# Linear attention and a mixture of experts on one core: attention in plain fp32 on halves of the tensor engine, and experts whose second layer runs five chunks behind the first

## The chip, the core and the metric

The kernel runs on one core of a Trainium2 chip. The metric is device microseconds from start to end of the program, smaller is better. A core has a tensor engine (PE) whose loads of the stationary operand stand as a row of their own (PEld), a vector engine (DVE), a scalar engine (ACT), GpSimd (POOL), and a sync engine (SP) that here issues most DMAs. Each engine works through its own instructions in order; semaphores hold them together.

## The reference

Two stages. Attention with a feature map: for 8 batches and 8 heads of 576 tokens by 64, both q and k become 256 features, exp(p) and exp(-p) of a projection p less its largest magnitude; no softmax over tokens.

```python
def phi(x):
    proj = np.einsum('bhsd,df->bhsf', x, w_phi)                 # 64 -> 128
    proj = proj - np.max(np.abs(proj), axis=-1, keepdims=True)
    return np.concatenate([np.exp(proj), np.exp(-proj)], axis=-1)
q_p, k_p = (phi(q), phi(k))
kv = np.einsum('bhsf,bhsd->bhfd', k_p, v)
z = np.sum(k_p, axis=2)
num = np.einsum('bhsf,bhfd->bhsd', q_p, kv)
den = np.einsum('bhsf,bhf->bhs', q_p, z)[..., None] + 1e-06
out = num / den
```

The result, as 4608 tokens of 512, goes through 8 experts, each token through one: the expert whose normalised embedding has the largest dot with the normalised token. The output is `gate * (relu(x @ w1[e]) @ w2[e])` with w1 512 x 1024, w2 1024 x 512, and gate the softmax weight of that expert. All in fp32.

## The kernel before

**Attention** runs in 16 quads: a quad is four heads of one batch, as two pairs (`X`) of two heads (`e`). The two heads of a pair lie on the two halves of the partitions, and the tokens of both pairs beside each other, 1152 columns or 9 blocks of 128. Matmuls with large outputs use fp32r operands, a rounded format that the tensor engine takes in one pass; to keep fp32's accuracy each operand is split into a rounded part (`h`) and what that leaves (`l`), and three products h·h, h·l, l·h are summed. So raw q, k, v and the key features kp are split: the rounding by ACT (L203) or DVE (L206), the rest by POOL or DVE (L197). In quad j:

- `proj` (L229): a block's projections for both heads of a pair at once, three fp32r products of 256 columns. DVE takes the largest magnitude (L233) and subtracts it (L235).
- For k, ACT makes the two exponentials (L242), then `split_k` splits them. For q, `qtr` turns the shifted projections on the tensor engine (L257), ACT makes the exponentials (L260).
- `kv` (L282): [v 1]ᵀ·kp, three fp32r products for each of five blocks; ACT copies it to SBUF (L285); `kve` (L296) turns it back with the identity and multiplies it with the embeddings in the same matmul, in fp32; DVE copies (L298).
- `num` (L310, L313): the numerators, the denominators and the dots with the embeddings of each block of tokens, plain fp32: 128 query features as the stationary operand, 73 columns. `norm` divides (L338 to L344), and writes x to DRAM.

Queue order is written out by hand for PE (`frame`); a scheduler orders the other engines. Numerators run a quad behind.

**Routing** (`route`, L405 to L443) counts the tokens of each expert and scatters them into a table, for groups of two batches beside the attention; the last group's runs after it, beside the first expert unit.

**Experts** run in 17 units, each of 2 slots of 128 tokens of one expert (3 in the first and in an expert's first unit where the number of slots is odd; 1 where the expert has one slot). Which code a unit runs is read from a table on the chip: `units` makes for every unit a Switch of 12 arms, each arm unrolled for one number of tokens, with or without the loads of the next expert. At a unit's end every engine loads the next arm's number (L132 on PE) and branches. In a unit `layers` goes through 8 chunks of 128 hidden features: `layer1` (L688, 12 fp32r matmuls of the unit's tokens), ACT's relu (L690) and DVE's rest (L693) into `hh`, `hl`, and one chunk later `layer2` (L711, three matmuls of 512 columns for each slot). A unit's tokens come by indirect DMA (`gather_parts`, L604), are turned by DVE (L617) and split (`xsplit`, L203, L648). The next expert's weights are split in the last unit of an expert (`next_w1`, `next_w2`, L584). A unit of one slot has its own code, `layers_of_slot` (L765, L774).

## Time and profile before

| | us |
|---|---|
| median of 3 runs (lowest, highest) | 1102.26 (1091.81, 1107.28) |
| the profiled execution, first to last instruction | 1133.1 |
| busy in it: PE, PEld | 965.3, 860.1 |
| busy in it: DVE, POOL, ACT | 651.2, 538.0, 433.5 |
| from its start to the first expert matmul | 516.1 |
| from there to the last expert matmul's end | 602 |

The profiled execution is a single one and is 2.8% longer than the median of the runs. Busy times of PE are modelled, since matmuls are pipelined: a matmul's row lasts from its start to the end of its result, so that neighbours overlap, and the distance of two starts is what one costs in a run of them. A plain fp32 matmul leaves two rows of LDWEIGHTS and MATMUL, an fp32r one a single row: `num`'s L310 stands in the program 512 times and has 992 rows with the tile np and 32 with bk. In brackets stands the idle time ahead of a row and what ended it; "issue" is a wait for nothing that the profile shows.

### The profile page before, as it was taken

What the parts mean: (1) busy time and instruction counts of PE and PEld (TensorE: products, weight loads), DVE (VectorE), ACT (ScalarE), POOL (GpSimd) and SP (SyncE); (2) the same over time, 40 slices, a digit from 0 to 9 for tenths busy, and PEclk for the clock granted to TensorE, in tenths of its full rate; (3) what the DMA queues carried; (4) which work ended last, traced back from release to release, by engine and by line L of the source; (5) the groups of instructions that cost most, each with busy time, mean ns of one, the idle gap of its engine ahead of it and who ended that gap; (6) DMA issues with size and microseconds to landing.
All of it is one profiled execution on the core that took longest, in us unless ns stands there. A gap on an engine that the chain in (4) does not pass through costs nothing. (4 is left out here: it accounts for less than half of the span.)

```text
span 1133.1 us, 17328 instructions
## 1 busy us (share of the span) xinstructions
PE 965.3 (85%) x6188; PEld 860.1 (76%) x6188; DVE 651.2 (57%) x1289; ACT 433.5 (38%) x841; POOL 538.0 (47%) x396
## 2 busy tenths in 40 slices
PE   6999999999899989988898788698687588798874
PEld 4899888888788878877787677587576477687763
DVE  8888898989899898969221223324225623422221
ACT  5556554645354554543221223314225413312221
POOL 5555564776477664655433224325144454422322
PEclk7999998999899999989899888799788778899887
DMA  5223221313132224111611111514313531511111
GB/s 166 83 66 106 61 88 46 105 51 106 63 105 66 79 90 180 45 29 43 215 37 49 38 40 49 191 23 126 106 45 116 159 123 46 188 28 45 47 35 43
DMA packets 55822, 94.22 MB, mean 83 GB/s; under 512 B 22471, under 2 KB 22855, under 8 KB 55440
## 3 DMA queue, kind: packets, MB, share of 16 engines
q1 hardware_dynamic: 45808, 68.97, 19.2%
q0 software_dynamic: 9632, 21.32, 6.3%
q14 instruction: 285, 2.33, 0.7%
q8 instruction: 97, 1.59, 0.7%
HBM read 70.64 MB, written 19.96 MB: 80 GB/s over the span
## 5 line engine op out<-in xcount | busy, mean ns | idle before, releaser
L604 POOL DMA_INDIRECT xg<-xd,ix x156 | 152.6, 978 | 260.2 <-DVE xt L617 168.5
L693 DVE SCALAR_TENSOR_TENSOR hl<-bk,hh 128x256 fp32r<-128x256 f32 (+2 forms) x128 | 57.6, 452 | 340.9 <-ACT hh L690 275.9
L197 POOL TENSOR_TENSOR kpl<-kp,kph 128x1024 fp32r<-128x1024 f32 (+1 forms) x79 | 170.1, 2153 | 121.3 <-DVE kph L206 111.7
L688 PE MATMUL bk<-xh,w1h 128*128 128x256 f32 (+4 forms) x512 | 169.5, 331 | 61.6 <-issue 54.2
L690 ACT ACTIVATE hh<-bk 128x256 fp32r<-128x256 f32 (+4 forms) x128 | 52.6, 415 | 346.4 <-PE bk L688 248.7
L688 PEld LDWEIGHTS bk<-xh,w1h 128*128 128x128 f32 x512 | 111.2, 217 | 73.4 <-issue 60.7
L688 PE MATMUL bk<-xl,w1h 128*128 128x256 f32 (+4 forms) x512 | 166.6, 325 | 0.0
L688 PE MATMUL bk<-xh,w1l 128*128 128x256 f32 (+4 forms) x512 | 165.9, 324 | 0.0
L260 ACT ACTIVATE qp<-bk 128x512 f32<-128x512 f32 (+1 forms) x160 | 79.9, 552 | 148.0 <-PE bk L257 134.5
L310 PE MATMUL np<-kvs,qp 128*128 128x73 f32 x992 | 126.1, 283 | 0.0
L310 PEld LDWEIGHTS np<-kvs,qp 128*128 128x128 f32 x992 | 124.2, 203 | 0.1
L688 PEld LDWEIGHTS bk<-xl,w1h 128*128 128x128 f32 x512 | 111.7, 218 | 4.9
L233 DVE TENSOR_REDUCE m<-bk 128x4 f32<-128x512 f32 (+1 forms) x157 | 98.9, 632 | 28.4 <-PE bk L229 22.6
L206 DVE CAST kph<-kp 128x1024 fp32r<-128x1024 f32 (+1 forms) x77 | 109.7, 1424 | 6.6 <-ACT kp L242 6.1
L688 PEld LDWEIGHTS bk<-xh,w1l 128*128 128x128 f32 x512 | 110.9, 217 | 0.0
L242 ACT ACTIVATE kp<-kd 128x512 f32<-128x512 f32 (+1 forms) x160 | 83.6, 580 | 50.2 <-DVE kd L235 49.5
L823 POOL DMA_INDIRECT out<-o,ent x39 | 41.0, 1052 | 95.5 <-ACT o L817 88.6
L711 PE MATMUL bk<-w2h,hh 128*128 128x512 f32 x136 | 59.7, 439 | 31.2 <-ACT hh L690 23.2
L711 PE MATMUL np<-w2h,hl 128*128 128x512 f32 (+1 forms) x160 | 65.7, 411 | 0.0
L711 PE MATMUL np<-w2h,hh 128*128 128x512 f32 (+1 forms) x160 | 65.4, 409 | 0.0
L711 PE MATMUL np<-w2l,hh 128*128 128x512 f32 (+1 forms) x160 | 65.2, 408 | 0.0
L257 PE MATMUL bk<-cst,qd 128*128 128x128 f32 x288 | 50.3, 296 | 8.9 <-DVE qd L235 8.9
(248 smaller groups left out, 2210.6 us busy)
## 6 DMA issues: line engine op xcount, KB each, us to landing
w1r<-w SPq DMA_DIRECT2D x14, 1024.0 KB
w2r<-w SPq DMA_DIRECT2D x14, 1024.0 KB
q<-qT SPq DMA_DIRECT2D x16, 576.0 KB
k<-kT SPq DMA_DIRECT2D x15, 576.0 KB
xd<-x SPq DMA_DIRECT2D x8, 1024.0 KB
va<-va SPq DMA_DIRECT2D x16, 325.0 KB
va<-va SPq DMA_DIRECT2D x16, 260.0 KB
xg<-xd,ix POOLq DMA_INDIRECT x156
```

The costliest lines, as they stand in the source:

```text
L197: ins = eng.tensor_tensor(out=hl[1], in0=raw, in1=hl[0].bitcast(F32), op=ALU.subtract)
L206: self.v.tensor_copy(out=out, in_=in_)
L233: v.tensor_reduce(out=m, in_=pv, axis=AX.X, op=ALU.max, apply_absolute_value=True)
L242: nc.scalar.activation(out=k[:, :nu, s], in_=d[:, :nu], func=AF.Exp, scale=sc)
L257: nc.tensor.transpose(out=ps[:, e, c, :], in_=self.dq[g][:, c, e, :], identity=self.ident)
L260: nc.scalar.activation(out=q[:, s, :, :nu], in_=ps[:, :, :nu], func=AF.Exp, scale=sc)
L310: nc.tensor.matmul(out=n[:, i * W:(i + 1) * W], lhsT=self.qp[g][:, s, e, c], rhs=self.kvs[j][:, X, e, s], start=(s == 0), stop=(s == 1))
L604: ins = nc.gpsimd.indirect_dma_start(out=self.xg[i][:, q * P:(q + 1) * P], out_offset=None, in_=self.xd.rearrange("n (g d) -> (n g) d", g= ...
L688: nc.tensor.matmul(out=ps, lhsT=w[:, d, fs], rhs=x[:, d, :n], start=(d == 0 and i == 0), stop=(d == 3 and i == 2))
L690: high = nc.scalar.activation(out=hh[:, :n], in_=ps, func=AF.Relu)
L693: low = self.v.scalar_tensor_tensor(out=out, in0=ps[:, cs], scalar=0.0, in1=hh[:, cs].bitcast(F32), op0=ALU.max, op1=ALU.subtract)
L711: self.nc.tensor.matmul(out=self.acc[a // P][:b - a], lhsT=h[:, a:b], rhs=w[:, c], start=(c == 0 and i == 0), stop=(c == 7 and i == 2))
```

## The change

Attention no longer splits anything. Every matmul of it takes plain fp32 operands and uses half of the array:

- `proj` works a head at a time: 64 rows of the array (partitions 0 to 63 for one head, 64 to 127 for the other), the two heads in turn, each into a PSUM bank of its own, 128 columns. A quad's 18 blocks go in five steps (`step`), over two pairs of banks.
- `kv` has the key features as the stationary operand, 64 of their 128 columns at a time, so that the outputs fall to partitions 0 to 63 and 64 to 127 in turn; moving are v, the ones, and v's products with the embeddings. These come from `vemb`, a new step (20 small matmuls a quad over a new input vT), copied by ACT into the tile `va`. `kve` and the copy `kt` go.
- `num` takes 64 tokens at a time in the same way. `norm` has one operation where it had two for the full and the half block.
- `split`, `split_v`, `split_k` and their work on ACT, DVE and POOL go. The loads of a quad are q, k, vT and va (zero padded to ten blocks of 73 columns). Of a batch pair's squares one more is taken; emb and tau are loaded by ACT's queue; table scatters and splits of the early expert's weights wait for DVE's latest subtraction.

In the experts every chunk has its own `hs` pair (three tiles and five that attention leaves), x has two sets, layer 1 goes round five PSUM banks, and `layer2` runs five chunks behind (`LAG`). An arm ends after chunk 4 of layer 2 (and, for a third slot, all chunks); chunks 5 to 7 of the first two slots and their outputs are in `unit_end`, code that is the same after every arm. It begins with the load of the next arm's number and a hint (`switch_hint`) that names the coming branch. A one-slot unit has no code of its own: it takes 256 columns in layer 1. The second half of w2 is split in an expert's first unit. There are 14 arms. Small `idle` instructions make the arms' counts equal. ACT, DVE, POOL and SP of the later units now stand in the written order too.

```diff
-    def split_k(self, g, copy=None, eng=None):
-        nu = GR[g][1]
-        k = self.kf[g][:, :nu]
-        hl = self.kp[g] = [t[:, :nu] for t in (self.pa.tile([P, 2, 2, 2, P], F32R, name="kp" + i, bufs=NK) for i in "hl")]
-        self.high(copy or self.dve_copy, hl, k)
-        self.last_k = self.low(eng or self.nc.gpsimd, hl, k)
...
+    def proj(self, j, parts, banks, step):
...
+        units = [(n, u) for n, us in parts for u in us]
+        k = len(units)
+        for i, (n, u) in enumerate(units):
+            for e in range(2):
+                r = slice(HD * e, HD * e + HD)
+                nc.tensor.matmul(out=banks[e][:, i * P:(i + 1) * P], lhsT=self.raw[j, n][r, u * P:(u + 1) * P], rhs=self.wp[r],
+                                 start=True, stop=True)
...
+    def step(self, j, s):
...
+        parts = (((1, range(4)),), ((1, [4]), (0, [4])), ((1, range(5, 9)),), ((0, range(4)),), ((0, range(5, 9)),))[s]
+        a = 2 * ((5 * j + s) % 2)
+        d = self.proj(j, parts, self.bk[a:a + 2], s)
...
+    def vemb(self, j, blocks):
...
+        ps = self.bk[5][:, 340:340 + NB * 2 * E]
+        for b in blocks:
+            for a in (0, 64):
+                self.nc.tensor.matmul(out=ps[a:a + 64, b * 2 * E:(b + 1) * 2 * E], lhsT=self.raw[j, 2][:, b * P + a:b * P + a + 64],
+                                      rhs=self.et[:, 2 * (j % 2) + b // 5].rearrange("p e x -> p (e x)"), start=True, stop=True)
...
     def kv(self, j, X, e):
...
+        for s in range(2):
+            c0 = (2 * e + s) * W
+            for i in range(5):
+                k = self.kp[j, X][e][:, s, i] if i < 4 else self.kp[j, 4][:, s, e]
+                for a in (0, 64):
+                    nc.tensor.matmul(out=self.bk[5][a:a + 64, c0:c0 + W], lhsT=k[:, a:a + 64],
+                                     rhs=self.va[j][:, 5 * X + i, e], start=(i == 0), stop=(i == 4))
...
     def num(self, j, X, e):
...
+        for i in range(5):
             for s in range(2):
...
+                for a in (0, 1):
+                    if i < 4:
+                        q = self.qp[j, X, e][:, s, i, 64 * a:64 * a + 64]
...
+                    nc.tensor.matmul(out=n[64 * a:64 * a + 64, i * W:(i + 1) * W], lhsT=q, rhs=kvs[:, s],
+                                     start=(s == 0), stop=(s == 1))
...
+    def layers(self, t, n, first, e):
...
+        for c in range(8 + CUT):
+            if c < 8:
+                self.layer1(t, c, max(n, 2 * P), (8 * t + c) % 5)
...
+            if LAG <= c < LAG + CUT:
+                self.layer2(c - LAG, n, slots)
...
+        for c in range(CUT, 8):
+            self.layer2(c, n, slots[2:])
+        if n > 2 * P:
+            self.output(t, n, 2)
...
+    def unit_end(self, t):
...
+        if t + 1 < NU:
+            self.arms[t + 1] = self.arm(t + 1)
+            self.tc.switch_hint(self.arms[t + 1], len(ARMS), label=f"unit{t + 1}")
+        self.done = []
+        for i in range(2):
+            for c in range(CUT, 8):
+                self.layer2(c, 2 * P, [i])
+            self.output(t, 2 * P, i)
...
-            for arm in self.tc.Switch({e: self.reg(t, 1, [e], 0, 11) for e in ENGINES}, 12):
-                self.unit(t, (P, 2 * P, 3 * P, 3 * P - 32, 3 * P - 64, 3 * P - 96)[arm // 2], arm % 2)
+            for arm in self.tc.Switch(self.arms[t], len(ARMS), hint=f"unit{t}"):
+                self.unit(t, *ARMS[arm])
+            self.unit_end(t)
```

What this makes of the order of instructions is shown at three places. First PE in the middle of a quad. Before, around one numerator step (tiles: np the numerators, kvs the key-value sums, qp the query features, wph and wpl the halves of the projection's weights, kh and kl those of k):

```order
L296 MATMUL bk_68<-ie,kt 128x73 x4
L257 MATMUL bk_65<-cst,qd 128x128 x4
L310 MATMUL np<-kvs,qp 128x73 x8
L313 MATMUL np<-kvs,qp 64x73 x2
L229 MATMUL bk_64<-wph,kh 128x256
L229 MATMUL bk_64<-wpl,kh 128x256
L229 MATMUL bk_64<-wph,kl 128x256
```

And of the change, the end of one `kv`, a numerator step and the projections behind it (kp the key features, d the shifted projections, qt raw q, wp the weights):

```order
L283 MATMUL bk_68<-va,kp_1051 64x73 x8
L283 MATMUL bk_68<-va,kp_1067 64x73 x2
L308 MATMUL np<-kvs,qp 64x73 x16
L308 MATMUL np<-kvs,q_100 64x73 x4
L257 MATMUL bk_67<-cst,d_1195 128x128 x4
L216 MATMUL bk_65<-wp,qt 128x128
L216 MATMUL bk_66<-wp,qt 128x128
```

A numerator step has 20 matmuls of 64 features where it had 8 of 128 and 2 of 64; a projection writes two banks in turn.

Second, DVE in a quad. Before, with the roundings of the key features (L206) and the rest of q (L197) between the reductions and subtractions:

```order
L235 TENSOR_TENSOR kd<-bk_63,m 128x512
L233 TENSOR_REDUCE m<-bk_64 128x4
L235 TENSOR_TENSOR qd<-bk_64,m 128x512
L206 CAST kph<-kp 128x1024
L233 TENSOR_REDUCE m<-bk_63 128x4
L235 TENSOR_TENSOR kd<-bk_63,m 128x512
L233 TENSOR_REDUCE m<-bk_64 128x2
L235 TENSOR_TENSOR kd<-bk_64,m 128x256
L197 TENSOR_TENSOR ql<-q_812,qh 128x1152
L206 CAST kph<-kp 128x1024
```

And of the change, a `norm` and the step behind it:

```order
L329 TENSOR_SCALAR rec<-np 128x10
L330 RECIPROCAL rec<-rec 128x10
L332 TENSOR_TENSOR dots<-np,rec 128x2x5x8
L332 TENSOR_TENSOR x<-np,rec 128x2x5x64
L224 TENSOR_REDUCE m<-bk_65 128x4
L224 TENSOR_REDUCE m<-bk_66 128x4
L226 TENSOR_TENSOR d_1173<-bk_65,m 128x512
L226 TENSOR_TENSOR d_1177<-bk_66,m 128x512
```

The reductions and subtractions stand as they did in number; between them there is only `norm` (and, every fourth quad, routing).

Third, PE from one expert unit to the next. Before, the last matmuls of an arm, the load of the next arm's number, the branch, and an arm's first matmuls:

```order
L711 MATMUL np<-w2l,hh_5534 128x512
L711 MATMUL np<-w2h,hl_5537 128x512
L1085 UNCONDITIONAL_BRANCH
L132 TENSOR_LOAD tab
L1085 SWITCH_STRIDE
L1085 ISA x2
L838 BRANCH_PREFETCH_HINT
L765 MATMUL bk_63<-w1h,xh 128x512
```

And of the change, from the end of an arm into `unit_end`, whose load and hint (L832) now stand ahead of 18 matmuls of layer 2, with the branch behind them:

```order
L1055 UNCONDITIONAL_BRANCH
L135 TENSOR_LOAD tab
L832 SWITCH_STRIDE
L832 ISA
L832 BRANCH_PREFETCH_HINT
L713 MATMUL bk_68<-w2h,qp 128x512
L713 MATMUL bk_68<-w2l,qp 128x512
```

The same load stands for the first of these units inside the first unit, ahead of its sixth chunk of layer 2.

More of the change, by code (lines that the diff above doesn't have):

```diff
@@ L454, in scatter @@
                 in_=ent[:, t, :], in_offset=None)
-            for split in (self.last, self.last_k):
-                self.after(ins, split, mybir.DependencyClass.NoSync, "the splits are waited for")
+            if bp < NT // 9 - 1:
+                self.after(ins, self.shift, mybir.DependencyClass.Sync, "one at a time")
             for other in self.scat:
@@ L480, in early @@
         e = self.reg(0, 4, [ET.SP], 0, E - 1)
[L481 to L483 removed]
+        for which in range(2):
+            for half in range(2):
+                self.wload(which, e, half)
     def early_slots(self):
@@ L831, in units, with first_unit, arm @@
+    def first_unit(self, extra):
+        self.done = []
+        self.first_layers(K * P, extra)
+        for i in range(K):
+            self.output(0, K * P, i)
+        self.gather_parts(2, range(2))
+    def arm(self, t):
+        return {e: self.reg(t, 1, [e], 0, len(ARMS) - 1) for e in ENGINES}
     def units(self, t):
@@ new lines, in quad, with turn, split, vemb @@
+    def quad(self, q):
+        cur, last = q < NQ, q == NQ
+        def turn(n=1):
+            for i in range(n):
+                self.pop(1)
+                self.square()
+        def split():
+            if q == NQ - 1:
+                self.w1_chunk()
+        def vemb(j, *blocks):
+            return self.vemb(j, range(*blocks)) if 0 < j < NQ else None
+        if cur:
+            self.load(q + 1, 1)
+            self.load(q + 1, 2)
+            self.load(q + 1, 0)
+        vemb(q, 0 if q == 1 else 4, 7)
+        if q:
+            self.kv(q - 1, 1, 0)
+        if q > 1:
+            self.num(q - 2, 1, 1)
+            self.norm(q - 2, 1)
+        turn()
+        if q:
+            self.qtr(q - 1, 1)
+        if cur:
+            self.step(q, 0)
+            self.step(q, 1)
+        turn(2)
+        if last:
+            for i in range(2):
+                self.w1_chunk()
+            self.kv(q - 1, 1, 1)
+            self.qtr(q - 1, 2)
+        elif q:
+            self.qtr(q - 1, 2)
+            done = vemb(q, 7, NB)
+            self.kv(q - 1, 1, 1)
+            if done:
+                done()
+        if cur:
+            self.load_v(q + 1)
+        if last:
+            return
+        if q:
+            self.num(q - 1, 0, 0)
+            self.num(q - 1, 0, 1)
+            self.norm(q - 1, 0)
+        turn()
+        if q:
+            self.qtr(q - 1, 3)
+        if q == 0:
+            self.embed(self.es)
+        self.step(q, 2)
+        if q == 0:
+            self.vemb(0, range(NB))()
+        self.step(q, 3)
+        split()
+        turn(2)
+        if q:
+            self.qtr(q - 1, 4)
+        if q:
+            vemb(q + 1, 0, 4)
+        else:
+            self.entries()
+        self.kv(q, 0, 0)
+        self.kv(q, 0, 1)
+        if q:
+            self.num(q - 1, 1, 0)
+        else:
+            self.nc.sync.dma_start(out=self.tbl.rearrange("(p n) c -> p n c", p=P), in_=self.pad)
+        turn(2)
+        self.qtr(q, 0)
+        self.step(q, 4)
+        split()
+        turn(2)
@@ L985, in pop @@
+            high, low = self.wsplit(0, self.chunks.pop(0))
+            self.after(high, self.shift, mybir.DependencyClass.Sync, "one at a time")
+            self.after(low, self.shift, mybir.DependencyClass.NoSync, "one at a time")
     def pop(self, n):
@@ L1014, in build @@
[L1014 to L1018 removed]
+        pool = self.ctx.enter_context(tc.tile_pool(name="w1", bufs=1, side="right"))
+        self.h1 = pool.tile([P, 4, F], F32R, name="w1h")
+        self.l1 = pool.tile([P, 4, F], F32R, name="w1l")
```

711 lines of the change are left out of this document (265 added, 446 removed).

## The prediction

> **What bounds the kernel now.** I read the busy time by stage first, then by group on DVE inside attention, then the distances of PE's rows, then PE's waits in the experts. By stage (us; busy time and rows of PE, PEld, DVE, ACT, POOL; granted clock; DMA share; GB/s):
>
> ```profile
> 0.00:58.00 58.00, 45.32 (x286) 39.51 (x287) 48.86 (x84) 30.03 (x51) 31.13 (x21) 0.82 0.38 123
> 58.00:427.00 369.00, 348.47 (x2765) 319.48 (x2766) 328.69 (x593) 192.60 (x371) 228.09 (x119) 0.97 0.25 79
> 297.70:420.50 122.80, 115.64 (x918) 105.90 (x918) 109.98 (x201) 63.77 (x123) 78.75 (x43) 0.97 0.25 79
> ...
> 516.00:560.50 44.50, 37.70 (x188) 33.26 (x185) 25.97 (x115) 10.14 (x22) 18.35 (x19) 0.95 0.39 123
> 560.50:1118.00 557.50, 450.86 (x2318) 392.67 (x2319) 172.74 (x327) 154.50 (x307) 206.40 (x203) 0.87 0.27 80
> 1118.00:1134.00 16.00, 1.18 (x3) 0.36 (x2) 0.00 (x0) 1.32 (x2) 2.03 (x2) 0.61 0.15 44
> ```
>
> Two programs stand one after the other. In attention (the third row is four quads, cut at the same place of the four-quad cycle: 30.7 us a quad) PE is busy for 94% and DVE for 90%: both are near their bound, and to take work from one alone would gain little. In the experts, 516 to 1118, DVE and ACT are idle for two thirds; PE has 602 us for 488.6 us of busy time, and the granted clock is 0.87 of full speed in most of it. What PE waits for there:
>
> ```profile
> PE bk L688 <- issue: 54.2, 14, 4.6
> PE bk L711 <- ACT hh L690: 23.2, 11, 3.8
> PE bk L711 <- issue: 8.1, 2, 4.0
> PE bk L688 <- ACT xh L203: 7.4, 1, 7.4
> PE np L706 <- issue: 5.5, 1, 5.5
> ```
>
> The first row is the start of a unit, about 3.9 us at 14 of 16 boundaries, with nothing to wait for but the branch. The second is layer 2 that follows its relu too closely. One boundary in order of time, with a stretch at full speed behind it:
>
> ```profile
> 598.78 0.36 PE L688 MATMUL bk<-xh,w1h 128*128 128x256 f32 x1 [3.06 <-issue]
> ...
> 603.68 0.67 PE L711 MATMUL bk<-w2h,hh 128*128 128x512 f32 x1 [1.78 <-ACT hh L690]
> 604.15 0.63 PE L711 MATMUL bk<-w2l,hh 128*128 128x512 f32 x1
> 604.57 0.63 PE L711 MATMUL bk<-w2h,hl 128*128 128x512 f32 x1
> ```
> ```profile
> 621.09 0.28 PE L688 MATMUL bk<-xh,w1l 128*128 128x256 f32 x1
> 621.21 0.29 PE L688 MATMUL bk<-xh,w1h 128*128 128x256 f32 x1
> ...
> 622.28 0.40 PE L711 MATMUL bk<-w2h,hh 128*128 128x512 f32 x1
> 622.51 0.40 PE L711 MATMUL bk<-w2l,hh 128*128 128x512 f32 x1
> ```
>
> Behind the idle 3.06 and 1.78 us the starts of L711 lie 0.43 to 0.47 us apart, at 622 they lie 0.23 apart: the idle time is paid twice, since the clock is halved after it. At full speed a 256-column matmul of layer 1 costs 0.12 us, one of layer 2 0.23.
>
> **The change part by part: attention.** On PE, a full quad has these matmuls after the change: 36 projections (18 blocks, two heads), 80 of `kv` (2 pairs, 2 heads, 2 signs, 5 blocks, 2 halves), 80 of `num`, 20 of `vemb`, 18 turns. All but the turns are plain fp32 and so leave two rows each. What such rows cost in a run:
>
> ```profile
> 233.45 0.28 PE L229 MATMUL bk<-wpl,qh 128*128 128x256 f32 x1
> 233.57 0.28 PE L229 MATMUL bk<-wph,ql 128*128 128x256 f32 x1
> 233.69 1.90 PE L310 MATMUL np<-kvs,qp 128*128 128x73 f32 x16
> 235.51 0.47 PE L313 MATMUL np<-kvs,qp 128*64 128x73 f32 x4
> ```
> ```profile
> 235.51 0.32 PEld L313 LDWEIGHTS np<-kvs,qp 128*64 128x64 f32 x4
> ```
> ```profile
> 236.96 0.66 PE L257 MATMUL bk<-cst,qd 128*128 128x128 f32 x4 [0.98 <-DVE qd L235]
> ```
> ```profile
> L310 PE MATMUL np<-kvs,qp 128*128 128x73 f32 x992 | 126.1, 283 | 0.0
> ...
> L257 PE MATMUL bk<-cst,qd 128*128 128x128 f32 x288 | 50.3, 296 | 8.9 <-DVE qd L235 8.9
> L313 PE MATMUL np<-kvs,qp 128*64 128x73 f32 x248 | 30.2, 246 | 0.0
> L313 PEld LDWEIGHTS np<-kvs,qp 128*64 128x64 f32 x248 | 20.6, 141 | 4.9
> ```
>
> A run lasts the distance of the starts times one less than its count, and one row. So L310 costs (1.90 - 0.28)/15 = 0.108 us a row, with 128 columns loaded; L313, with 64, (0.47 - 0.25)/3 = 0.073 by its matmuls and (0.32 - 0.14)/3 = 0.06 by its loads. I take 0.065, nearer the loads, since a short run holds its slow start. A turn costs (0.66 - 0.30)/3 = 0.12. From the last start of L310 (233.69 + 1.62 = 235.31) to the first of L313 there are 0.20 us, 0.09 more than between two of L310: that much is lost as the array goes from whole to half.
>
> If the half-array matmuls took turns, a quad would cost PE 72 x 0.108 = 7.8 (projections), 320 x 0.065 = 20.8 (`kv`, `num`), 40 x 0.06 = 2.4 (`vemb`), 18 x 0.12 = 2.1 (turns), and 12 changes between whole, row halves and column halves at 0.09 = 1.1: 34.2 us, more than the 28.9 it has now (115.64/4). If the two halves, which always come in turn, run side by side, the first three terms halve: 15.5 + 2.1 + 1.1 = 18.7 us. No row of before shows two halves in turn (L313 stays on one half), so these are the two bounds. I take the lower: the two matmuls of a pair read no common stationary data, write other partitions or another bank, and neither waits for the other.
>
> The Trainium skill's page "TensorEngine Tiling (Array Packing)", section Key Properties, says that tiles work independently, loads and matmuls of different tiles in parallel, and that a change of the tiling mode drains the engine; by it the sum is the lower one, and the drain agrees with the 0.09 us.
>
> DVE must follow. Its groups over the twelve quads of 58 to 427:
>
> ```profile
> L206 DVE CAST kph<-kp 128x1024 fp32r<-128x1024 f32 (+1 forms) x60 | 85.7, 1428 | 5.4 <-ACT kp L242 5.0
> ...
> L197 DVE TENSOR_TENSOR ql<-q,qh 128x1152 fp32r<-128x1152 f32 x12 | 27.3, 2278 | 0.0
> L342 DVE TENSOR_TENSOR x<-np,rec 128x512 f32<-128x512 f32 x24 | 16.4, 684 | 0.2
> L298 DVE COPY kvs<-bk 128x292 f32<-128x292 f32 x24 | 10.8, 451 | 0.4 <-PE bk L296 0.3
> ...
> L413 DVE TENSOR_SCALAR r_rn<-r_rn,rtau 128x9 f32<-128x9 f32 x3 | 7.0, 2341 | 0.1
> L344 DVE TENSOR_TENSOR x<-np,rec 64x128 f32<-64x128 f32 x24 | 6.8, 284 | 0.2
> ```
>
> L206, L197 and L298 go: 123.8/12 = 10.3 us a quad. In `norm` the half-block operations (L344, 6.8 and about 4 for the dots) go and the large ones grow by a quarter (4.1 and about 1): about -0.5 a quad. Of 328.69/12 = 27.4 that leaves 16.6, and routing steps like L413, 2341 ns for nine columns, should shorten when POOL no longer splits beside them. DVE is under PE by 2 us; ACT loses five copies a quad and keeps its exponentials, under its 16 of now (192.60/12). Loads grow from 1.7 to 2.5 MB a quad (q and k 0.58 each, vT 0.64, va 0.73), with x's stores 3.1 MB in 20 us, 152 GB/s; 79 GB/s take a share of 0.25, so 0.48: on SP they are issued a quad ahead, and this hides them. The table scatters and weight splits that now wait for a subtraction hold up only POOL's next scatter and exponentials that need the same subtraction; I price them at nothing, at a subtraction (0.6 us) each if that cover fails.
>
> To PE's 18.7 I add the idle time of now, (122.8 - 115.64)/4 = 1.8: 20.5 us a quad for 30.7. The first stretch (58 us, to the turns of quad 1) holds the same waits for first loads, and DVE's 48.86 busy us there lose a third: 45. Fourteen quads to 488: 14 x 20.5 = 287 for 430. The end (488 to 516: last numerators, first tokens turned) is a chain across engines, I keep 23 of 28. The first expert matmul comes at 45 + 287 + 23 = 355, for 516.
>
> **The experts.** The arithmetic stays. Layer 1 has 96 matmuls in each of 16 units, with 4640 columns over the units (ten of 256, two each of 384 and 352, one each of 320 and 288): at 0.12 us for 256 columns and in proportion, 96 x 4640/256 x 0.12 = 209 us at full speed. Layer 2 has 920 at 0.23: 212. With 8 for the one-slot unit and the turns, before needs 429. The change adds 96 x 0.12 = 11.5 for the one-slot unit's 256 columns and 12 x 0.23 = 2.8 for its empty slot, less the 6 of its own code: 437.
>
> The relu's wait goes with five chunks of distance and five banks: the longest was 3.8 us, and five chunks of layer 1 are 5 x 12 x 0.12 = 7.2. At a boundary, PE's load and hint stand ahead of 18 x 0.23 = 4.2 us of matmuls, and the longest start wait is 4.6: that cover holds all or nearly all of it, and I leave 0.5 us at each of 16. What comes late next is, first, unit 1:
>
> ```profile
> 515.79 0.55 DVE L338 TENSOR_SCALAR rec<-bk 128x4 f32<-128x4 f32 x3
> 516.08 0.44 PE L688 MATMUL bk<-xh,w1h 128*128 128x384 f32 x1
> ```
> ```profile
> 537.85 0.15 DVE L565 TENSOR_SCALAR tab<-t_sel 128x1 int32<-128x1 f32 x1
> ```
> ```profile
> 546.20 0.95 POOL L595 DMA_INDIRECT xg<-xd,ent  x1 [0.30 <-issue]
> ```
> ```profile
> 555.03 0.49 ACT L203 ACTIVATE xh<-bk 128x384 fp32r<-128x384 f32 x1 [1.75 <-PE bk L677]
> ```
>
> From the last `norm` (515.79) over the table to unit 1's tokens takes 40 us, while the first unit has 96 x 0.18 + 72 x 0.23 = 33.8 us of matmuls; the chain is unchanged: 6 us. PE's load of the arm's number, now within this unit some 27 us after its start, waits for the row at 537.85, 22 us after it: covered, by 5 us. Second, the expert with one slot leaves 20 us for 4 MB of the next weights: 200 GB/s where the busiest slices moved 226: I allow 6 us. For half clock after these waits 4. So 437 + 8 + 6 + 6 + 4 = 461 for 602.
>
> Together 355 + 461 and the last 15 us (unchanged) are 831 us against the profiled 1133.1. The median of the runs stands at 1102.26/1133.1 = 0.973 of that: **809 us**.
>
> **The rivals.** *The halves take turns.* If a column half's load cannot run beside the other half's matmul, `kv`, `num` and `vemb` stay at 23.2 and only the projections (row halves) halve: 23.2 + 3.9 + 2.1 + 1.1 + 1.8 = 32.1 us a quad, 11.6 more, over 15 quads 174: 1005, or 978 measured. If the row halves do not run side by side either: 36.0 a quad, 1063, or 1034. For it: loads, at 0.06 us a row, are as dear as matmuls here, so one shared load path is enough. Against: nothing in the rows, which hold no such pair. 8% and 10%.
>
> The Trainium skill's page "TensorE: Matmul & The Clock Gate", section "What overlaps and what doesn't" in Part 3, says that a load overlaps running matmuls only where the row group differs; column halves share their rows, so by that rule this rival's first form comes. No run so far shows it.
>
> *The unit's start stays.* If the hint comes too late or is dropped, 16 x 3.9 = 62 us return, and about 3.4 us of half clock at each (54): 831 + 116 - 8 = 939, or 914 measured. For it: the wait is not explained by any row but "issue". 10%. With a form of the rival above together 1083 to 1140, around no change: 4%.
>
> *Slower: every change of half drains.* If the 0.09 us is lost at every one of the 216 half-array matmuls, 19.4 us join 36.0: 55.4 a quad, 35 more, 15 times: 1355, or 1318 measured. It decides for slower from a quad of 42 us, which is 0.03 us a matmul beyond taking turns. For it is that one gap; against, that L313's four rows on one half show it only once. 5%.
>
> **How the numbers follow.** My forecast has 63%, with its own range of 770 to 855 (from no idle time in the quads to 24 us a quad and 1 us more at each boundary). About 2% is the least that a measurement tells from no change, 1080 to 1124. Faster: 63 + 18 + 10 = 91, less a little for one-sided mishaps: 0.90; same 0.04; slower 0.06. The range holds 8 in 10 from 770 to 1000: the forecast, the late start, and the first form of taking turns; all-serial halves, both rivals and the drain stay outside.
>
> **What would show it.** Right: a quad near 20 us; starts of `num`'s rows (L308) 0.03 to 0.04 us apart on average; DVE at 16 to 17 us a quad; no L203, L206, L197 rows in attention; the "issue" waits of layer 1 (now L691) under 10 us in all; granted clock near 1 in the experts; first layer 1 at 345 to 370. Wrong: L308 rows 0.06 or more apart, a quad of 30 us or more, start waits of 3 us and more with 0.43 us rows of layer 2 behind them, or waits of PE for DVE or the loads that take several us in every quad.

## The result, and the profile after

The changed kernel takes 811.28 us (median of 4 runs, 809.27 to 811.81) where the kernel before takes 1104.77: a ratio of 0.737, with a 95% interval of 0.732 to 0.742. The profiled execution spans 810.0 us. Where the runs of a kernel fall into a faster and a slower state, a ratio and its interval are worked out from the fast ones, a median from all. The forecast was 809, but part of that closeness is luck, as the last of the experiments show.

By stage (us; busy time and rows of PE, PEld, DVE, ACT, POOL; granted clock; DMA share; GB/s): start, fourteen quads, four quads of them, the end of attention, the first expert unit, and the other sixteen.

```profile
0.00:41.00 41.00, 32.29 (x606) 30.00 (x606) 23.80 (x66) 18.24 (x38) 2.65 (x7) 0.88 0.69 247
41.00:316.00 275.00, 270.38 (x6301) 249.23 (x6298) 213.04 (x495) 171.98 (x396) 35.87 (x34) 1.00 0.52 169
158.20:236.50 78.30, 77.48 (x1807) 71.37 (x1804) 60.36 (x137) 49.20 (x113) 10.57 (x10) 1.00 0.51 166
316.00:333.00 17.00, 15.49 (x331) 13.80 (x330) 11.45 (x33) 11.25 (x25) 3.93 (x5) 1.00 0.02 3
333.00:374.40 41.40, 37.70 (x192) 33.58 (x188) 26.14 (x113) 14.59 (x31) 21.70 (x21) 0.96 0.35 104
374.40:800.40 426.00, 410.36 (x2397) 365.62 (x2395) 190.09 (x509) 171.82 (x437) 202.45 (x187) 0.98 0.35 107
```

A quad takes 275/14 = 19.6 us for 30.7, with PE busy for 98% of it (270.38/275) and DVE for 15.2 us (213.04/14): PE alone now bounds attention. The first layer 1 comes at 333 us for 516, a gain of 183 us; the prediction's own sign for it, 345 to 370, was too late, and its 16 to 17 us for DVE too long. From there to PE's end it is 467 us for 602, a gain of 135. The granted clock in the units after the first is 0.98, where most of the experts had 0.87.

What PE waits for in the whole expert part (each line: the waiting matmul's output and program line, what ended the wait, us in total, times, the longest):

```profile
PE bk L691 <- DVE hl L696: 11.3, 4, 4.0
PE bk L691 <- DVE hh L696: 4.5, 1, 4.5
...
PE bk L691 <- issue: 0.2, 1, 0.2
```

Both large rows of before are gone: layer 1's 54.2 us for "issue" at 14 unit starts is 0.2 us, and layer 2 (now L713) waits for no relu at all. In their place stands a wait that the prediction did not have, layer 1 waiting for DVE's low part of the hidden layer (L696), that is for a free PSUM bank, 15.8 us.

### The profile page after: what moved, and what is told of

Read it like the earlier page. It is cut to its first block, busy times and chain, and to the rows that moved or that the text cites. A ratio compares the mean times of both kernels' runs of the same rounds, so it can differ in the third digit from the quotient of the medians.

```text
span 810.0 us, 24715 instructions
## 1 busy us (share of the span) xinstructions
PE 766.2 (95%) x9812; PEld 692.2 (85%) x9812; DVE 464.5 (57%) x1215; ACT 388.6 (48%) x924; POOL 268.6 (33%) x254
## 4 chain that ended last, share of the span: by engine, by line
PE 76%; ACT 10%; issue 6%; DVE 4%; DMA 1%; ACTq 0%; POOL 0%; DVEq 0%; POOLq 0%
PE bk L691 22%; PE acc L713 13%; PE bk L713 10%; PE bk L283 9%; PE np L308 8%; PE bk L216 6%; PE bk L257 5%; PE bk L269 3%; ACT sq L357 3%; ACT kp L232 2%; ACT qp L232 2%; ACT xh L202 1%; DVE w1l L577 1%; DMA xg<-xd,ix 1%; ACT w2h L202 1%
## 5 line engine op out<-in xcount | busy, mean ns | idle before, releaser
L691 PE MATMUL bk<-x,w1h 128*128 128x256 f32 (+3 forms) x512 | 105.7, 302 | 4.0 <-DVE hl L696 2.1
L696 DVE SCALAR_TENSOR_TENSOR hl<-bk,hh 128x256 fp32r<-128x256 f32 (+2 forms) x51 | 22.0, 449 | 146.9 <-ACT hh L693 146.8
L691 PE MATMUL bk<-xh,w1h 128*128 128x256 f32 (+3 forms) x288 | 87.7, 304 | 13.7 <-DVE hl L696 9.2
L283 PE MATMUL bk<-va,kp 128*64 128x73 f32 x2560 | 92.5, 229 | 1.5 <-DVE run L436 1.5
L691 PEld LDWEIGHTS bk<-x,w1h 128*128 128x128 f32 x512 | 85.3, 192 | 7.6 <-DVE hl L696 2.4
L283 PEld LDWEIGHTS bk<-va,kp 128*64 128x64 f32 x2560 | 86.4, 138 | 2.3 <-DVE run L436 1.7
L691 PE MATMUL bk<-xh,w1l 128*128 128x256 f32 (+3 forms) x288 | 86.6, 301 | 0.0
L691 PE MATMUL bk<-xl,w1h 128*128 128x256 f32 (+3 forms) x288 | 86.4, 300 | 0.0
L226 DVE TENSOR_TENSOR d<-bk,m 128x512 f32<-128x512 f32 x128 | 81.9, 681 | 0.0
L691 PE MATMUL bk<-x,w1l 128*128 128x256 f32 (+3 forms) x256 | 77.0, 301 | 0.0
L308 PE MATMUL np<-kvs,qp 128*64 128x73 f32 x1984 | 74.0, 226 | 0.0
L713 PE MATMUL acc<-w2h,qp 128*128 128x512 f32 (+2 forms) x172 | 62.0, 394 | 0.0
```

Source lines behind the costliest of these rows:

```text
L226: self.shift = v.tensor_tensor(out=d, in0=ps, in1=m.unsqueeze(2).broadcast_to([P, k, P]), op=ALU.subtract)
L283: nc.tensor.matmul(out=self.bk[5][a:a + 64, c0:c0 + W], lhsT=k[:, a:a + 64], rhs=self.va[j][:, 5 * X + i, e], start=(i == 0), stop=(i == 4))
L308: nc.tensor.matmul(out=n[64 * a:64 * a + 64, i * W:(i + 1) * W], lhsT=q, rhs=kvs[:, s], start=(s == 0), stop=(s == 1))
L691: nc.tensor.matmul(out=ps, lhsT=w[:, d, fs], rhs=x[:, d, :n], start=(d == 0 and i == 0), stop=(d == 3 and i == 2))
L713: self.nc.tensor.matmul(out=self.acc[i][:h.shape[1]], lhsT=h, rhs=w[:, c], start=(c == 0 and k == 0), stop=(c == 7 and k == len(parts) - 1))
```

## The experiments

The runs fell on several chips, and these are not alike: each set is therefore read against the time of the kernel before on its own chip. The first four ran where that takes 1103 us.

**Do the two halves run side by side?** First the column halves, one after the other. In `num` the edit is this (the same in `kv` and `vemb`):

```diff
-        for i in range(5):
-            for s in range(2):
-                for a in (0, 1):
+        for a in (0, 1):
+            for i in range(5):
+                for s in range(2):
```

> kv, num and vemb with the loop over the two column halves outside, so that one half's matmuls come one after the other (5 to 10 in a row) before the other half's. Same matmuls, same loads, same results. Theory (column halves run side by side only because they come in turn): the rows of kv and num lie 0.065 us apart for 0.033 now, 360 rows a quad x 0.032 = 11.5 us a quad, 16 quads: about 811 + 185 = 995 us, a quad of 31 us for 19.6. Rival (a 64-column fp32 matmul simply costs 0.033 us in a long run, in whatever order the halves come; the 0.06 of before was a slow start): 811 us, a quad of 19.6.

It took 898.5 us. The fourteen quads, in the windows of that run, and a stretch of PE's rows in order of time:

```profile
48.90:402.70 353.80, 353.80 (x6298) 333.58 (x6297) 213.90 (x496) 173.65 (x397) 35.85 (x34) 1.00 0.40 131
```
```profile
101.34 0.26 PE L283 MATMUL bk<-va,kp 128*64 128x73 f32 x1
101.37 0.27 PE L269 MATMUL bk<-et,vt 128*64 128x16 f32 x2
101.43 1.86 PE L283 MATMUL bk<-va,kp 128*64 128x73 f32 x36
```

A quad is 353.80/14 = 25.3 us, 5.7 more, with the same matmuls: the order alone decides, and the rival falls. But the price is half of what was expected. Where `kv` puts five matmuls (ten rows) on a half before it changes, a row costs (1.86 - 0.26)/35 = 0.046 us; inside `num`, with twenty rows on a half, the median distance of two rows is 0.063 and the mean 0.057. Read so, a row of 64 columns waits for the one before it on its own half, 0.06 us, and where a run on one half ends, the first rows of the other already run beside its last ones. In the rows above, one of L283 starts between rows of L269 that stand ahead of it in the queue.

The row halves, by the same means:

```diff
-        for i, (n, u) in enumerate(units):
-            for e in range(2):
+        for e in range(2):
+            for i, (n, u) in enumerate(units):
```

> The projections with the loop over the two heads (row halves) outside: 4 or 2 matmuls on one half, then as many on the other. Theory (row halves side by side because they come in turn): the 72 rows of a quad go from 0.061 to about 0.108 us, 3.4 us a quad, 16 quads: about 811 + 54 = 865 us. Rival (the order of the row halves does not matter; the 64-row load is cheap by itself): 811 us.

It took 836.7 us. One step of eight projections, then the quads:

```profile
110.02 1.71 PE L216 MATMUL bk<-wp,qt 64*128 64x128 f32 x16
```
```profile
45.60:346.10 300.50, 295.90 (x6299) 275.00 (x6297) 218.14 (x482) 174.24 (x394) 35.72 (x34) 1.00 0.47 155
```

In the changed kernel, where the halves come in turn, a step of projections and one of `num`:

```profile
119.46 1.16 PE L216 MATMUL bk<-wp,qt 64*128 64x128 f32 x16
...
122.22 1.19 PE L308 MATMUL np<-kvs,qp 128*64 128x73 f32 x32
```

The same sixteen rows of projections last 1.16 us there: (1.71 - 0.28)/15 = 0.095 us a row for (1.16 - 0.28)/15 = 0.059. A quad is 300.50/14 = 21.5 us, 1.8 more, again about half of what was expected, probably since two runs of eight rows still overlap where they meet.

How finely must the halves be mixed? The last run on this question puts two matmuls on a half, then two on the other, in `num` alone:

```diff
             for s in range(2):
-                for a in (0, 1):
+            for a in (0, 1):
+                for s in range(2):
```

> In num alone, two matmuls on one column half, then two on the other (10 in a row on each in the run with the column halves apart, 1 in the changed kernel). Theory (a row waits only for the row before it on its own half, and PE looks a few rows ahead: in that run kv's 5 in a row cost 0.046 us a row, num's 10 in a row 0.057): runs of two cost no more than in turn, 0.033 to 0.036 us a row, within 8 us of the changed kernel on the same chip. Rival (each repeat of a half costs a whole row's time): (0.033 + 0.062)/2 = 0.048 us a row, 160 rows x 0.015 = 2.4 us a quad, 38 us more.

It took 856.9 us on a chip where the changed kernel takes 865.1. Its `num` rows:

```profile
102.43 1.24 PE L308 MATMUL np<-kvs,qp 128*64 128x73 f32 x32
```

That is (1.24 - 0.23)/31 = 0.033 us a row; the changed kernel's 32 rows above take 1.19 us, 0.031. Two matmuls in a row on one half cost next to nothing, five cost half of the gain in those rows, ten most of it.

**What took the start wait away?** The prediction named the early read of the arm and the branch hint, with 18 matmuls behind them. First without any hint:

```diff
-            self.tc.switch_hint(self.arms[t + 1], len(ARMS), label=f"unit{t + 1}")
...
-            for arm in self.tc.Switch(self.arms[t], len(ARMS), hint=f"unit{t}"):
+            for arm in self.tc.Switch(self.arms[t], len(ARMS)):
```

> The branch hint is left out ahead of every unit; the early read of the arm and the 18 layer-2 matmuls behind it stay. Theory (the hint is what removed the start wait of PE): 3.9 us of wait return at about 16 starts, and some 3 us of half clock behind each: 811 + 62 + 50 = about 920 us, with rows of layer 1 that wait for 'issue'. Rival (the early read of the arm alone does it): 811 us. Between: the wait of the engines' code is there, but in part hidden: 840 to 890 us.

It took 809.4 us, so the hint does not carry the gain. At one start of sixteen it does something: PE's branch into the first unit after the opening one, with the hint and without, and PE's first matmul there without it. (PEldq is PE's sequencer; a row has the duration as min/median/max in ns, then first and last start in us.)

```profile
L1055 PEldq COMPARE_BRANCH  x1: 359/359/359, 370.9 to 370.9; - x1
```
```profile
L1053 PEldq COMPARE_BRANCH  x1: 6306/6306/6306, 371.5 to 371.5; - x1
```
```profile
378.09 0.93 PE L691 MATMUL bk<-x,w1h 128*128 128x352 f32 x2 [2.93 <-issue]
```

There the hint stands 7 us ahead of the branch, which takes 0.36 us with it (0.35 to 0.36 in all eleven runs that have the hint there) and 6.3 without, 2.9 of them as idle time. At the later starts it stands 2.5 to 3.3 us ahead of the longer branches, and they take 3.3 to 5.3 us with it and 3.4 to 4.0 without. Why it works only at the first was not tested.

What hides the long branches is seen in PE's own queue. One of them, of before and after:

```profile
L1085 PEldq COMPARE_BRANCH  x2: 326/2364/4403, 593.0 to 594.1; - x2
```
```profile
L1055 PEldq COMPARE_BRANCH  x1: 3587/3587/3587, 447.7 to 447.7; - x1
```

The branch takes 4.4 us in the one and 3.6 in the other. What differs is how much work is already in PE's queue when the branch is reached. Of before and of after, in order of time:

```profile
594.18 0.39 PE L711 MATMUL np<-w2h,hh 128*128 128x512 f32 x1
...
595.32 0.40 PE L711 MATMUL np<-w2h,hl 128*96 128x512 f32 x1
598.78 0.36 PE L688 MATMUL bk<-xh,w1h 128*128 128x256 f32 x1 [3.06 <-issue]
```
```profile
447.82 0.63 PE L713 MATMUL bk<-w2h,qp 128*128 128x512 f32 x2
...
451.30 0.40 PE L713 MATMUL acc<-w2h,q 128*128 128x512 f32 x1
451.53 0.33 PE L691 MATMUL bk<-xh,w1h 128*128 128x256 f32 x1
```

Before, 6 matmuls were still to start when the branch began at 594.1; after, 16 were, from 447.82 to 451.30, and layer 1 follows 0.23 us behind the last of them. Over all branches of PE that take more than 1.5 us, 0 to 13 matmuls start while the branch lasts before (median 2), and 14 to 17 after. Two more runs vary that number. The arm read late:

```diff
-            self.arms[t + 1] = self.arm(t + 1)
-            self.tc.switch_hint(self.arms[t + 1], len(ARMS), label=f"unit{t + 1}")
         for i in range(2):
             for c in range(CUT, 8):
                 self.layer2(c, 2 * P, [i])
             self.output(t, 2 * P, i)
+        if t + 1 < NU:
+            self.arms[t + 1] = self.arm(t + 1)
+            self.tc.switch_hint(self.arms[t + 1], len(ARMS), label=f"unit{t + 1}")
```

> The arm's number is read, and the hint given, behind the 18 matmuls of the common end, next to the branch, as the kernel before did; the 18 matmuls stay. If the early read is what hides the start: 3 to 4 us of wait at each start return, 870 to 920 us. If the 17 matmuls in PE's queue hide it: the read adds about 0.7 us to the 3.6 to 4.4 us of the branch, 0.3 to 0.7 us at 16 starts: 815 to 825 us.

And no matmuls in the common end (`CUT` 8 in place of 5, all of layer 2 inside the units' own code; the read of the arm then stands next to the branch too):

> All of layer 2 stays inside a unit's own code; behind the common end's read of the arm and the hint there are no matmuls left, only the outputs; distance and banks stay. The sum's step (the 18 matmuls behind the early read hide the start): 3.9 us of wait at each of 16 starts and half clock behind them return, 900 to 930 us. A second theory, from the profile after (PE's branch takes 3.6 to 4.4 us before and after the change alike, and PE's queue holds some 17 matmuls, 4 us, that are issued ahead of it; the wait is hidden wherever nothing stops the issue of the last matmuls): the read and one more jump take about 1 us more than the queue holds, 16 x 1.1 = 18 us and a little half clock, 830 to 845 us.

These two ran where the kernel before takes 1134 us. There was no run of the changed kernel on that chip; on a third, where the kernel before takes 1138, it takes 865.1 (852.3 to 868.8). The late read took 854.5 us, within that; without matmuls in the end it was 871.6. Each is a single run. What can be told apart are the starts. One start of each, the late read first:

```profile
509.43 0.48 PE L691 MATMUL bk<-x,w1h 128*128 128x256 f32 x2 [0.88 <-ACT o L807]
```
```profile
531.53 0.41 PE L691 MATMUL bk<-xh,w1h 128*128 128x352 f32 x1 [1.76 <-issue]
```

Beyond the 0.23 us of a matmul, the sixteen starts cost 2.7 us together in the changed kernel (2.2 on the third chip), 11.5 with the late read (12 matmuls during the branch, by the median) and 25.6 without the matmuls (9). Neither brings back the 54 us of before: of the two theories for the end without matmuls the second, 18 us, comes close, and the first, 62, falls. That the rest of before's wait comes from its layer 2 is argued from the rows and not tested: a matmul that waits for the relu holds up what stands behind it in PE's queue, the branch too. Before, only six matmuls follow the last relu of a unit of two slots; at five of the sixteen starts PE waits 1.4 to 3.9 us for that relu just ahead of them, and at fourteen no more than six matmuls start while the branch lasts.

**The distance of layer 2.** Two chunks in place of five, on the chip with 1134:

```diff
     def layers(self, t, n, first, e):
+        LAG = 2
```

> Layer 2 follows layer 1 by two chunks in place of five in the units from the second on; the first unit, the five banks, the kept chunks and the common end stay, so that between the last chunk of layer 1 and a unit's end there are fewer matmuls of layer 2. Theory A (the distance is what hides the relu: 23 us of waits of layer 2 for it before, 0 now, and half clock behind each): these waits return and with them most of the half clock, 835 to 850 us, with rows of layer 2 that wait for hh or hl. Theory B (two chunks are already more than the relu takes, 1.6 us from a chunk's first matmul, since 2 x 12 x 0.12 = 2.9 us of layer 1 and some of layer 2 lie between; what hid it badly before was the number of banks): 811 to 815 us.

It took 901.2 us. PE's waits there, and one of them with the rows behind it:

```profile
PE bk L713 <- ACT hh L693: 21.5, 8, 5.5
PE bk L713 <- ACT q L693: 12.2, 3, 5.1
```
```profile
549.35 0.80 PE L713 MATMUL bk<-w2h,hh 128*128 128x512 f32 x1 [4.55 <-ACT hh L693]
549.94 0.63 PE L713 MATMUL bk<-w2l,hh 128*128 128x512 f32 x1
```

From the first layer 1 to PE's end it is 526 us. The same stretch is 477 and 491 us in the two runs of the third chip that have the changed kernel's experts, and 482 in the late-read run on this run's own chip, so the edit costs some 35 to 48 us: by its time theory A, at its upper end or above it. 33.7 us of waits for relus come back and, as in the last row, matmuls at half clock behind them: layer 2's starts that lie 0.33 to 0.5 us apart add 15 us over 0.232 each (under 3 in the changed kernel).

But the waits do not lie where theory A has them. 18.0 of the 21.5 us in the first row are four waits right behind the start of a new expert, as the one shown, where ScalarE itself is late; that is looked at next. The 12.2 us of the second row are three waits for the last chunk of the unit ahead of a new expert. ScalarE and SP there:

```profile
533.26 0.38 ACT L693 ACTIVATE q<-bk 128x256 fp32r<-128x256 f32 x1 [4.15 <-remote]
```
```profile
525.45 0.39 SPq L570 DMA_DIRECT2D w1r<-w  x1
526.09 0.39 SPq L570 DMA_DIRECT2D w2r<-w  x1
```

The relu's own layer 1 has ended at 528.8, and "remote" means that the profile finds nothing that released it. What else the edit moves is at work here: the load of half of w2, the splits of w2 and the preparation of later tokens go by `LAG` too and come three chunks earlier, so that two loads of 1 MB are issued together inside the unit, and the queues that carry instructions have no packet from 528.2 to 533.5 us. Elsewhere the longest waits for a relu are 1.6 and 1.1 us: two chunks nearly cover the relu itself, as theory B says. So the other three chunks cover ScalarE's late spots in the main, and some of these the edit itself made: the price of the distance alone stays open.

**Why ScalarE is late.** The new wait for banks, in ScalarE's rows around one start of a new expert (layer 1 began at 497.2), PE's row, and the weight loads that SP issues just then:

```profile
508.99 0.82 ACT L693 ACTIVATE hh<-bk 128x352 fp32r<-128x352 f32 x2 [6.71 <-issue]
```
```profile
510.13 0.66 PE L691 MATMUL bk<-xh,w1h 128*128 128x352 f32 x1 [3.10 <-DVE hl L696]
```
```profile
497.78 0.39 SPq L570 DMA_DIRECT2D w2r<-w  x1
498.41 1.22 SPq L570 DMA_DIRECT2D w1r<-w  x1
```

ScalarE has nothing to wait for but its own instructions, as PE had before the change; it has no sixteen long matmuls in its queue. The DMA queues from 498.4 to 503.7 us, by packets, MB and share:

```profile
q1 hardware_dynamic: 706, 1.41, 80.2%
q0 software_dynamic: 32, 0.07, 3.2%
```

The queues that carry instructions, which have 14 packets in 20 us around a start without weight loads (420 to 440 us), do not appear for 5.3 us. So the two loads were moved from the last steps of a unit into the next one:

```diff
                 if first and c == 5:
-                    self.wload(1, self.reg(t - 1, 0, [ET.SP], 0, E - 1), 1)
+                    old = self.reg(t - 1, 0, [ET.SP], 0, E - 1)
+                    self.wload(0, old, 1)
+                    self.wload(1, old, 0)
+                    self.wload(1, old, 1)
```

> Two loads of 1 MB (the second half of w1, the first half of w2, both of the expert after the next) are issued in the sixth step of an expert's first unit in place of the last steps of the unit before; nothing else changes. What it tests: at the start of the first unit of experts e7, e0, e1 and e4 ScalarE's first relu comes 10.2 to 11.7 us after layer 1 begins, at the other starts 1.6 to 3.7 us (8.1 and 6.0 at two more), PE runs out of free banks and waits 3.4, 4.8, 4.2 and 2.4 us. Theory (ScalarE's code comes by DMA and stands behind these 2 MB, which the trace shows moving just then, with no packet of the code's queue for 5.4 us): the late relus and PE's waits go, 15 us and some 2 us of half clock: 794 to 798 us. Rival (an arm with other code than the last takes ScalarE that long whatever else moves): 811 us, same waits. A loss is possible at the expert with one slot, which then waits longer for its successor's weights (2.2 us now): up to 10 us back.

It took 803.6 us (six runs, 800.4 to 806.2). ScalarE at the same start, layer 1 having begun at 498.7, the queues with instructions from there to 505 us, and PE's waits from 333 us on:

```profile
505.26 0.82 ACT L693 ACTIVATE hh<-bk 128x352 fp32r<-128x352 f32 x2 [1.60 <-PE bk L691]
```
```profile
q14 instruction: 7, 0.06, 3.4%
q8 instruction: 1, 0.02, 1.0%
```
```profile
PE bk L713 <- ACT qp L693: 7.3, 1, 7.3
PE bk L691 <- DVE hl L696: 3.1, 2, 2.2
```

The "issue" wait in front of the relu is gone and the relu comes 6.6 us after layer 1 in place of 11.8; at the other three starts 6.7 to 7.4 for 10.4 to 11.3. The waits for banks fall from 15.8 to 3.1 us. So the weights did hold up ScalarE, by 3 to 5 us at each, and with them gone five banks cover most of what is left; that it is ScalarE's code that they hold up is read from the missing packets. Why 6.6 us remain, against 1.7 to 3.7 at most other starts, is open. The gain is 8 us and not 15, mostly because of the new 7.3 us in the first row, behind the one-slot unit, whose half of w2 now comes too late:

```profile
629.00 0.63 ACT L202 ACTIVATE w2h<-w2r 128x512 fp32r<-128x512 f32 x1 [10.86 <-DMA w2r<-w]
```

All six runs lie below the four of the changed kernel, on chips whose times of the kernel before agree within 0.2%; the ratios to before, 0.733 (0.728 to 0.737) and 0.737 (0.732 to 0.742), do not separate them. A further run issued both loads in the first step of the expert's first unit:

> As with the weights issued in the sixth step of an expert's first unit, but in its first step, w2's half ahead of w1's. There ScalarE waited 7 us in the unit after the one-slot unit for a half of w2 that came late. Theory (the code of the next unit must only not stand behind weights at the branch, and the weights are then early enough for the one-slot unit): the late relus stay away and that wait goes or falls under 3 us: 796 to 801 us. Rival (loads in the first step hold up the rest of the unit's code as before): relus late again inside these units, 805 to 812 us.

It took 848.9 us where the kernel before takes 1134, a ratio of 0.749 (0.743 to 0.755); the changed kernel's on the third chip is 0.755 (0.748 to 0.761). The relus at those four starts come 7.1 to 9.4 us after layer 1, between the two other placings, and PE still waits 8.2 us for relus. It is not told apart from the changed kernel.

**The chip.** That the second set of kernels had attention 27 us longer, which none of them touches, asked for the changed kernel again, and for a second profile of the kernel before.

> The changed kernel as it is. The kernel before took 1103 us on the chip of the first four runs and 1134 on that of the next four, and attention alone, which those kernels leave as it is, took 27 us longer there, in quads where PE waits for its own instructions. If that is the chip and no effect of the edits, the changed kernel's time goes with the kernel before's: about 811 us where that takes 1103, about 836 to 845 where it takes 1134; then the late read of the arm cost 10 to 18 us, the end without matmuls 27 to 35, two chunks of distance 57 to 65. Otherwise it stays at 811 wherever it runs.

> The kernel before as it is, for a second profile. The prediction multiplied its sum by 0.973, the ratio of the runs' median 1102 to the profiled execution's 1133. If that profile came from a slower chip: where the runs of the kernel before take 1103 us, its span is 1095 to 1112, and a quad whose end holds table scatters takes 31 us as the others, in place of 33.9; the factor is then that of a chip and does not belong in the sum. If profiling itself costs 3%: a span of 1130 to 1140 beside runs of 1103.

The chip for these was a third, with 1138 us for the kernel before. The changed kernel took 865.1 us (ratio 0.755), where the expectation had 836 to 845: its time goes with the chip, and by more than the kernel before's. The costs that the expectation worked out from those numbers for the late read, the end and the distance fall with them. The second profile of the kernel before spans 1135.3 us beside runs of 1138: profiling costs nothing that shows. (The expectation had a chip of 1103 us in view, which this was not.) The profile on which the prediction rests was then very likely from a chip of the slower sort too: it spans 1133.1 us beside runs of 1102, and its first layer 1 comes at 516 us for 518 in the second. A profile of the kernel before on a faster chip was not taken. In the changed kernel's profile on the third chip, two quads by windows, and the same two on the first chip:

```profile
139.30:166.00 26.70, 23.11 (x450) 20.62 (x450) 13.88 (x28) 13.84 (x34) 5.80 (x6) 0.87 0.42 144
166.00:185.10 19.10, 19.10 (x454) 17.69 (x450) 13.88 (x28) 10.67 (x23) 0.00 (x0) 1.00 0.42 138
```
```profile
138.40:158.20 19.80, 19.35 (x454) 17.81 (x450) 13.89 (x28) 13.69 (x33) 5.21 (x6) 1.00 0.60 194
158.20:177.40 19.20, 19.20 (x454) 17.72 (x451) 13.89 (x28) 10.66 (x23) 0.00 (x0) 1.00 0.43 138
```

Of these two the one with six table scatters on POOL (the last column but three) is longer by 7 us; the other agrees within 0.1. Three such quads and the end of attention (22.5 us for 17) hold most of the 27 us. In them, PE waits in this way:

```profile
145.02 0.36 PE L283 MATMUL bk<-va,kp 128*64 128x73 f32 x4 [1.09 <-issue]
```

A last run took the scatters out of the quads, all of them behind the last one:

> The table scatters of the first groups, which GpSimd issues beside the quads (6 in quads 6, 10 and 14, one or two in others), are all issued behind the last quad; the same work, the same result. Two chips so far took 27 us longer in attention than the first, in just the quads with six scatters (26.4 and 26.7 us; 19.1 and 20.0 in those with none or one), with PE waiting for its own instructions there. Theory (on such a chip PE gets its instructions late while GpSimd issues indirect DMAs): where the kernel before takes 1130 us or more, all full quads take 19 to 20.5 us and the first layer 1 begins at 335 to 345 plus what the moved scatters hold up at the end, which are 30 or so at 1.28 us each. Rival (these chips are slow at those places for another reason, such as the stores of x that fall into the same quads): those quads stay at 26 us. Where the kernel before takes about 1103 us, the quads are 19 to 20 us either way and this tells nothing.

It fell on a chip where the kernel before takes 1097 us. Its quads are 19 to 20 us, as they are with the scatters on the first chip, so it says nothing on the cause. It took 839.1 us, since the first tokens are gathered behind the scatters: PE waits 33.7 us for them ahead of the first expert unit.

## Why the prediction was right, and where only its sum was

**Attention, the forecast against taking turns: right, shown.** `num`'s rows lie 0.032 us apart on average (0.03 to 0.04 had been named), and the two runs with the halves apart show that this is the order's doing. The Trainium skill's page "TensorE: Matmul & The Clock Gate", section "What overlaps and what doesn't" in Part 3, by which a load overlaps only where the row group differs, would have given the rival for the column halves; the measurement decides against it here, since column halves share all rows and still cost 0.032 us a row in turn against 0.063 on one half. The rival of a drain at each half falls with it.

**The terms of attention.** PE's 18.7 us a quad is 19.4 (77.48/4), in part since a projection's row costs 0.059 and not 0.054, 0.4 us over 72 rows. The 1.8 us of idle time that was carried over is 0.2: those waits were mostly for DVE, which has 4 us to spare now (15.2 us; 16.6 had been worked out). The routing step of 2341 ns, which was to shorten once POOL no longer splits beside it, takes 231 ns. The start is 41 us for the 45, the end 17 for the 23 that were kept of 28. Together 333 for 355.

**The experts: a sum whose errors cancel, and a step named wrongly in part.** The experts take 467 us for the 461. PE's matmuls at their usual distances come to 433 us for the 437. For unit starts, unit 1's tokens and the one-slot expert's weights 20 us had been allowed, and 2.7 were needed: unit 1 starts 0.24 us behind the last matmul ahead of it, and 1.9 of the 2.7 us are at the unit behind the one-slot one, where a branch of 5.3 us and the split of the unit's tokens end last, not the weights. Against that, half clock costs some 12 us for the 4 allowed (rows over a quarter later than usual with no idle time ahead of them: 8.7 us in layer 1, 3.2 in layer 2), and there are 15.8 us of waits for banks that the sum did not have. That it came out only 6 us low is luck.

The step "PE's load and hint stand ahead of 18 x 0.23 = 4.2 us of matmuls" gave the right cover for a partly wrong reason: the hint is worth 2.9 us at one start, so the rival that lost 62 us if it was dropped falls. The cover is the queue: PE's branch still takes 3.3 to 5.3 us at ten starts, behind 14 to 16 matmuls that wait for nothing. The early read adds three or four to them (12 with the late read), and it and the matmuls of the common end together are worth some 23 us. With layer 2 two chunks behind, the starts cost 6.5 us for 2.7. No run takes away all of it at once, so that these add up to the 54 us of before is not shown.

**What was missed.** The list of what is late next held unit 1's tokens and the one-slot expert's weights, not ScalarE's own start. PE's queue covers PE's branch; ScalarE has no such cover, and at four new experts it starts late while 2 MB of weights are loaded: 13.6 us of PE's waits for banks from the second unit on.

**The factor of 0.973.** The sum of 831 us was made for the profiled execution and then multiplied by the runs' median over its span. That ratio was read as one between a profile and its runs; very likely it was one between two kinds of chip. On the slower kind the changed kernel takes 862 us in its profile: there the sum was 31 us low, 5 in attention and 30 in the experts (491 us for 461), with the tail 4 the other way. On the faster kind it takes 810, and there the sum was 21 us high, which the factor took back: the 809 owes its closeness to that. The ratio of the two kernels, forecast at 809/1102 = 0.734, is 0.737 on the one and 0.755 on the other.

## What to carry to other kernels

Small matmuls on two halves of the array should be written in turn, or at most two on a half at a time: here that is worth about half of their time, and long runs on one half lose it, though nothing else changes. PE's branch was hidden where its queue held independent work for as long as the branch takes and nothing in that work waited; so place matmuls whose inputs are long finished right in front of the branch, and look at every other engine that takes the same branch, and at large loads that are issued at that moment. An edit of one constant can move loads as well: look in the trace at what else it moved before its time is put down to the constant's name. A profile and the runs beside it may come from different chips; compare their spans in a stage that can't differ before a ratio between them goes into a sum.

## What the runs showed that was not expected

- In the changed kernel PE takes 3.3 to 5.3 us for the branch into a unit in ten of sixteen cases (0.3 to 0.4 in the others), and 14 to 16 matmuls of 512 columns that were issued before it start while it lasts.
- A hint 7 us ahead of the branch made it 0.36 us for 6.3; 2.5 to 3.3 us ahead it made no difference. What decides was not tested.
- Chips differ by 3.8% for the kernel before (1097 to 1138 us) and by 6.6% for the changed one (811 to 865). The part of it that lies in attention is in the quads with six table scatters and at attention's end. There, and in the experts (14 us of "issue" waits for 0.2), PE waits for its own instructions; the cause was not found.
